# Storing four neighbouring rows of the second-layer weights in a partition, and reading every fourth column of the first layer, in a gated-attention and mixture-of-experts kernel

## The chip, the cores and the metric

One core of a Trainium2 chip. The metric is the device time of one launch in microseconds (us). Versions are compared over executions on the same chip, in alternating rounds.

## The reference

```python
def _attn_ref(q, k, v, f_logit):            # (4, 8, 768, 48) each
    f = 1.0 / (1.0 + np.exp(-f_logit))
    for t in range(S):
        state = f[:, :, t, :, None] * state + np.einsum('bhd,bhe->bhde', k[:, :, t], v[:, :, t])
        y[:, :, t] = np.einsum('bhd,bhde->bhe', q[:, :, t], state)

def _moe_ref(x, domain_probs, w1, w2):      # x (3072, 384), w1 (4, 384, 1024), w2 (4, 1024, 384)
    p = domain_probs / (domain_probs.sum(-1, keepdims=True) + 1e-09)
    for e in range(E):
        h = np.maximum(x @ w1[e], 0.0)
        out += p[:, e:e + 1] * (h @ w2[e])
```

The attention runs in chunks of 128 steps; its output, transposed to `xT`, is the input of the experts. F = 1024 is the hidden width, and any permutation of F is allowed as long as w1's columns and w2's rows agree.

## The kernel before

All weights stay in SBUF as bf16. Row `ko * 128 + ki` of w2 lies in partition `ki`, so one contiguous run is one row: 384 elements, 768 bytes when stored. w1 lies with D in the partitions, and a matmul takes 128 neighbouring columns as stationary operand. The first weights come in pieces: each of the experts 0 and 1 has its w1 in two halves of 512 columns, expert 0 its w2 in two halves too.

```python
    w1_sb = wpool.tile([128, E, KD, F], BF16)
    w2_sb = wpool.tile([128, E, KF, Din], BF16)
    w1_r = moe_w1.rearrange("e (ko ki) f -> e ki ko f", ki=128)
    w2_r = moe_w2.rearrange("e (ko ki) d -> e ki ko d", ki=128)
    # ... cut ...
    def load_w(i, e, which, ks, cols):
        w, r = (w1_sb, w1_r) if which == 1 else (w2_sb, w2_r)
        ins["w", i] = nc.gpsimd.dma_start(out=w[:, e, ks, cols], in_=r[e][:, ks, cols])
    # ... cut ...
    def mm_h(c, e, fc, n0, n1, nf):
        for f in range(nf):
            for kk in range(KD):
                nc.tensor.matmul(out=hp(c, e, fc, n0, n1, nf)[:, f], lhsT=w1_sb[:, e, kk, (fc + f) * 128:(fc + f + 1) * 128],
                                 rhs=tl("xT", c)[:, kk, n0:n1], start=(kk == 0), stop=(kk == KD - 1))
    # ... cut ...
    pieces = [(e, 1, every, slice(i * F // 2, (i + 1) * F // 2)) for e in range(2) for i in range(2)]
    pieces += [(0, 2, slice(i * KF // 2, (i + 1) * KF // 2), every) for i in range(2)]
    pieces += [(e, which, every, every) for e, which in ((2, 1), (1, 2), (3, 1), (2, 2), (3, 2))]
    # ... cut: for every piece i
        op = P.add(f"w {i}", {"DMA": 2.05 if i < 6 else 4.4}, lambda _: None, ..., deps=[iss], lag=1.0)
```

The kernel places its work itself: a plan in Python takes an estimate of each operation's time (the 2.05 and 4.4 us above are such) and fixes the order in which every engine gets its instructions. The waits between engines are set afterwards by the framework, from which tiles and which parts of them each instruction reads and writes.

## Time and profile before

| | before |
|---|---|
| median time | 298.5 us (3 runs), 298.61 us with the runs beside the changed kernel (6) |
| span of the profiled run | 296.6 us |
| TensorE busy | 289.0 us, 97% |
| first w1 matmul, last matmul start | 19.75 us, 292.98 us |
| packets of the queue that loads weights | 11248: 4096 of 768 bytes for w2, 1536 of 1024 and 768 of 2048 bytes for w1 |

In the views, PE is TensorE's matmuls, PEld its weight loads, DVE is VectorE, ACT ScalarE, POOL GpSimd, and q0 the queue that loads the weights. L374 is line 374 of the kernel's file.

TensorE sets the end, so the way to read this profile is by the starts of its matmuls: their spacing, and each place where a spacing is longer than its shape needs. One more piece of the timeline of TensorE matters later, the start of the expert work (start, duration, engine, line, tiles, form, count):

```profile
19.11 0.81 PE L644 MATMUL ps_m<-busy 128*128 128x512 bf16 x3
19.75 0.82 PE L374 MATMUL ps_m<-xT,w_sb 128*128 128x256 bf16 x6
20.41 0.33 PE L365 MATMUL ps_t<-ident,yb 128*128 128x128 bf16 x3
```

Six 256-column matmuls on w1 run without a break, right after three filler matmuls, which work on constant data and whose results nobody reads. The first half of w1 of expert 0 had landed at 19.10 us, the second landed at 21.98 us, and at 19.75 us nothing needs it yet.

### The profile page before, as it was taken

How to read it: one execution, taken by the hardware profiler on the slowest of the kernel's cores; microseconds unless marked ns; L12 is line 12 of the kernel's file. 1: busy time of each engine (PE TensorE's matmuls, PEld its weight loads, DVE VectorE, ACT ScalarE, POOL GpSimd, SP SyncE). 2: the span in 40 equal slices, each digit the busy share in tenths (PEclk: the TensorE clock that was granted, in tenths of full speed). 3: DMA queues.
4: the chain of work that ended last, by engine and by line, in shares of the span. 5: the costliest groups of instructions: out<-in, count | busy, mean ns of one | idle time of the engine just before them, and what ended most of it. 6: DMA issues, size and time to landing. Idle time of an engine off the chain costs nothing.

```text
span 296.6 us, 5591 instructions
## 1 busy us (share of the span) xinstructions
PE 289.0 (97%) x2172; PEld 170.0 (57%) x2172; DVE 126.1 (43%) x250; ACT 174.3 (59%) x317; POOL 106.1 (36%) x180
## 2 busy tenths in 40 slices
PE   6899999999999999999999999999999999999995
PEld 2476555567777775555555555555555555555553
DVE  6786012785763673045375235243523222101223
ACT  5656656666684667777477575554475544465440
POOL 5786401138767448144449372243220000000000
PEclk9999999999999999999999999999999999999999
DMA  7999999998979999998979932102432100200002
GB/s 157 200 169 206 207 192 210 189 210 167 201 152 166 191 171 185 209 187 164 198 133 218 179 60 35 27 0 67 122 61 30 27 2 27 80 2 0 0 2 106
DMA packets 136462, 36.43 MB, mean 123 GB/s; under 512 B 126812, under 2 KB 135644, under 8 KB 136436
## 3 DMA queue, kind: packets, MB, share of 16 engines
q1 hardware_dynamic: 125188, 29.35, 52.0%
q0 software_dynamic: 11248, 6.72, 16.4%
q8 instruction: 17, 0.28, 0.4%
q14 instruction: 9, 0.07, 0.1%
HBM read 31.51 MB, written 4.72 MB: 122 GB/s over the span
## 4 chain that ended last, share of the span: by engine, by line
PE 78%; DMA 14%; POOL 3%; SPq 2%; issue 1%; ACT 1%; DVE 0%; POOLq 0%
PE ps_m L389 37%; PE ps_m L374 35%; DMA w_sb<-in_moe_w_dram 10%; DMA k<-in_k_dram 4%; SPq L237 2%; POOL w_sb L246 2%; PE ps_t L325 2%; PE ps_t L340 1%; PE ps_t L336 1%; PE ps_t L273 1%; POOL vb L233 1%; PE ps_t L346 1%; ACT e L293 1%; DVE o L396 0%; ACT xT L226 0%
## 5 line engine op out<-in xcount | busy, mean ns | idle before, releaser
L385 ACT ACTIVATE h<-ps_m 128x512 bf16<-128x512 f32 (+2 forms) x188 | 102.4, 548 | 91.9 <-PE ps_m L374 88.9
L374 PE MATMUL ps_m<-xT,w_sb 128*128 128x512 bf16 (+3 forms) x708 | 152.8, 339 | 0.6 <-ACT xT L226 0.6
L389 PE MATMUL ps_m<-w_sb,h 128*128 128x384 bf16 (+1 forms) x776 | 152.6, 324 | 0.1
L389 PEld LDWEIGHTS <-h 128*128 128x128 bf16 x776 | 75.0, 98 | 59.0 <-DMA w_sb<-in_moe_w_dram 0.3
L396 DVE SCALAR_TENSOR_TENSOR o<-ps_m,pn,o 128x384 f32<-128x384 f32 (+1 forms) x73 | 44.5, 612 | 117.3 <-PE ps_m L389 111.1
L374 PEld LDWEIGHTS <-w_sb 128*128 128x128 bf16 x708 | 65.3, 98 | 43.5 <-issue 0.7
L301 POOL TENSOR_TENSOR qk<-q,e 128x384 bf16<-128x384 f32 x18 | 21.4, 1195 | 36.5 <-ACT e L293 34.3
L360 POOL TENSOR_TENSOR Sf<-Sf,egs 48x192 f32<-48x192 f32 x40 | 20.2, 504 | 36.5 <-DVE Sf L353 34.4
L329 DVE TENSOR_TENSOR AT<-ps_t,mask 128x512 bf16<-128x512 f32 x48 | 30.2, 683 | 5.1 <-PE ps_t L325 5.1
L383 DVE TENSOR_SCALAR h<-ps_m 128x256 bf16<-128x256 f32 (+2 forms) x40 | 19.3, 499 | 26.5 <-PE ps_m L374 13.1
L293 ACT ACTIVATE e<-ps_t 128x384 f32<-128x384 f32 x48 | 26.7, 668 | 5.0 <-PE ps_t L273 3.5
L301 POOL TENSOR_TENSOR qk<-k,e 128x384 bf16<-128x384 f32 x20 | 20.2, 1013 | 8.7 <-ACT e L293 5.5
L353 DVE TENSOR_TENSOR Sf<-Sf,ps_t 48x192 f32<-48x192 f32 x40 | 14.0, 350 | 10.3 <-PE ps_t L346 9.4
L246 POOL DMA_DIRECT2D w_sb<-in_moe_w_dram x11 | 8.8, 807 | 18.5 <-DMA k<-in_k_dram 17.2
L361 POOL CAST sb<-Sf 48x192 bf16<-48x192 f32 x40 | 13.6, 340 | 2.6
L398 ACT ACTIVATE o<-ps_m,pn 128x384 f32<-128x384 f32 x22 | 12.8, 582 | 2.5 <-PE ps_m L389 1.5
L644 PE MATMUL ps_m<-busy 128*128 128x512 bf16 x34 | 10.9, 423 | 1.5 <-DVE busy L144 1.5
L265 ACT ACTIVATE ex<-f 128x768 f32<-128x768 f32 (+1 forms) x14 | 10.4, 746 | 1.8 <-DMA f<-in_f_logit_dram 1.8
L298 POOL DMA_DIRECT2D egs<-e x16 | 9.0, 563 | 6.9 <-ACT e L293 6.9
L340 PE MATMUL ps_t<-vb,AT 128*128 128x48 bf16 x192 | 11.4, 184 | 0.0
L269 ACT ACTIVATE gp<-ex 128x768 bf16<-128x768 f32 (+1 forms) x14 | 10.5, 751 | 0.3
L340 PEld LDWEIGHTS <-AT 128*128 128x128 bf16 x192 | 9.9, 97 | 1.1
(54 smaller groups left out, 120.6 us busy)
## 6 DMA issues: line engine op xcount, KB each, us to landing
out_dram<-o SPq DMA_DIRECT2D x23, 192.0 KB, 2.0
w_sb<-in_moe_w_dram POOLq DMA_DIRECT2D x5, 768.0 KB, 18.0
k<-in_k_dram SPq DMA_DIRECT2D x10, 384.0 KB, 5.6
q<-in_q_dram SPq DMA_DIRECT2D x10, 384.0 KB, 5.5
v<-in_v_dram SPq DMA_DIRECT2D x10, 384.0 KB, 5.7
f<-in_f_logit_dram SPq DMA_DIRECT2D x9, 384.0 KB, 4.6
w_sb<-in_moe_w_dram POOLq DMA_DIRECT2D x6, 384.0 KB, 9.0
f<-in_f_logit_dram SPq DMA_DIRECT2D x6, 192.0 KB, 3.8
```

Of the source, the lines that this page charges most:

```text
L246: ins["w", i] = nc.gpsimd.dma_start(out=w[:, e, ks, cols], in_=r[e][:, ks, cols])
L293: nc.scalar.activation(out=o, in_=i, func=AF.Exp, scale=1.0 if j else -1.0)
L301: engines[eng].tensor_tensor(out=tl("qk", c, b)[:, j, :, 0:D].rearrange("t (i r) d -> t i r d", r=2), in0=tl("qk"[j], c, b // 2)[:, hh(b), ...
L329: nc.vector.tensor_tensor(out=tl("AT", c, b)[:, r].rearrange("s i t -> s (i t)"), in0=tl("A", c, b, r).rearrange("s i t -> s (i t)"), in1= ...
L340: nc.tensor.matmul(out=y[:, h * D:(h + 1) * D], lhsT=AT[:, r, i, :], rhs=vb[:, h, :], start=(c == 0), stop=True, skip_group_check=True)
L353: nc.vector.tensor_tensor(out=Sf[rows, b], in0=Sf[rows, b], in1=KV[rows, :, r, :], op=ALU.add)
L360: nc.gpsimd.tensor_tensor(out=Sf[rows, b], in0=Sf[rows, b], in1=eg, op=ALU.mult)
L374: nc.tensor.matmul(out=hp(c, e, fc, n0, n1, nf)[:, f], lhsT=w1_sb[:, e, kk, (fc + f) * 128:(fc + f + 1) * 128], rhs=tl("xT", c)[:, kk, n0: ...
L383: nc.vector.tensor_relu(out=dst, in_=src)
L385: nc.scalar.activation(out=dst, in_=src, func=AF.Relu)
L389: nc.tensor.matmul(out=tl("op", c, e, nt, part)[:, cols], lhsT=tl("h", c, e, half_of(c, nt * T))[:, fc, nt * T:(nt + 1) * T], rhs=w2_sb[:, ...
L396: nc.vector.scalar_tensor_tensor(out=o, in0=op, scalar=pe, in1=o, op0=ALU.mult, op1=ALU.add)
```

## The change

The intent is larger packets for w2, so that the weights come sooner: partition `ki` holds the rows `s * 512 + ki * 4 + j`, j = 0 to 3, whose four rows are one run of 3072 bytes. For h to come out in the same order, chunk `fc = 4 s + j` of w1 has to be the columns `s * 512 + j`, `+ 4`, `+ 8` and so on. The plan's estimates change with it. (Here and below an edit is shown in part: unchanged lines and some changed ones are left out, and `...` stands for a part of a line.)

```diff
-    w2_r = moe_w2.rearrange("e (ko ki) d -> e ki ko d", ki=128)
+    w2_r = moe_w2.rearrange("e (s ki j) d -> e ki s j d", ki=128, j=KF // 2)
     def load_w(i, e, which, ks, cols):
-        w, r = (w1_sb, w1_r) if which == 1 else (w2_sb, w2_r)
-        ins["w", i] = nc.gpsimd.dma_start(out=w[:, e, ks, cols], in_=r[e][:, ks, cols])
+        dst, src = w1_sb[:, e, ks, cols], w1_r[e][:, ks, cols]
+        if which == 2:
+            dst = w2_sb[:, e].rearrange("ki (s j) d -> ki s (j d)", j=KF // 2)[:, ks]
+            src = w2_r[e].rearrange("ki s j d -> ki s (j d)")[:, ks]
+        ins["w", i] = nc.gpsimd.dma_start(out=dst, in_=src)
+    def f_cols(fc):
+        s, j = divmod(fc, KF // 2)
+        return slice(s * F // 2 + j, (s + 1) * F // 2, KF // 2)
-                nc.tensor.matmul(..., lhsT=w1_sb[:, e, kk, (fc + f) * 128:(fc + f + 1) * 128],
+                nc.tensor.matmul(..., lhsT=w1_sb[:, e, kk, f_cols(fc + f)],
-    pieces += [(0, 2, slice(i * KF // 2, (i + 1) * KF // 2), every) for i in range(2)]
+    pieces += [(0, 2, slice(i, i + 1), every) for i in range(2)]
-        op = P.add(f"w {i}", {"DMA": 2.05 if i < 6 else 4.4}, ...)
+        op = P.add(f"w {i}", {"DMA": (2.1 if i < 6 else 4.3) if which == 1 else 1.7 if i < 6 else 3.5}, ...)
```

More of the change, by code (lines that the diff above doesn't have):

```diff
@@ L373, in mm_h @@
             for kk in range(KD):
-                nc.tensor.matmul(out=hp(c, e, fc, n0, n1, nf)[:, f], lhsT=w1_sb[:, e, kk, (fc + f) * 128:(fc + f + 1) * 128],
+                nc.tensor.matmul(out=hp(c, e, fc, n0, n1, nf)[:, f], lhsT=w1_sb[:, e, kk, f_cols(fc + f)],
                                  rhs=tl("xT", c)[:, kk, n0:n1], start=(kk == 0), stop=(kk == KD - 1))
@@ L443 @@
                     -600 + 3 * i, deps=issued[-1:] + ([ld[1, "k", 0]] if i == w_last else []))
-        op = P.add(f"w {i}", {"DMA": 2.05 if i < 6 else 4.4}, lambda _: None, -400 if i == w_last else -460 + i, deps=[iss], lag=1.0)
+        op = P.add(f"w {i}", {"DMA": (2.1 if i < 6 else 4.3) if which == 1 else 1.7 if i < 6 else 3.5}, lambda _: None, -400 if i == w_last else -460 + i, deps=[iss], lag=1.0)
         issued.append(iss)
```

## The prediction

In the prediction, rival (a) is that strided weight loads are slow enough to hold up the matmuls.

> **What bounds the kernel now.** I read four views, from coarse to fine. The page first: the busy times, and the span in 40 slices.
>
> ```profile
> span 296.6 us, 5591 instructions
> ...
> PE 289.0 (97%) x2172; PEld 170.0 (57%) x2172; DVE 126.1 (43%) x250; ACT 174.3 (59%) x317; POOL 106.1 (36%) x180
> ...
> PE   6899999999999999999999999999999999999995
> ...
> DMA  7999999998979999998979932102432100200002
> ```
>
> TensorE is busy for 97% of the span, and the DMA engines are nearly full for the first 23 slices of 7.4 us. The change touches both: it makes second-layer weight (w2) transfers cheaper and it alters how TensorE reads first-layer weights (w1). So the question is which of the two sets the end. A busy TensorE may be a slow one, so the next view is the timeline of TensorE in the stage where the weights arrive (start, duration, engine, line, tiles, form):
>
> ```profile
> 34.02 0.81 PE L374 MATMUL ps_m<-xT,w_sb 128*128 128x512 bf16 x3
> 34.67 0.81 PE L389 MATMUL ps_m<-w_sb,h 128*128 128x384 bf16 x4
> 35.32 0.81 PE L374 MATMUL ps_m<-xT,w_sb 128*128 128x512 bf16 x3
> 35.97 0.81 PE L389 MATMUL ps_m<-w_sb,h 128*128 128x384 bf16 x4
> ```
>
> Each group starts 0.65 us after the last: three 512-column matmuls (0.65 / 3 = 216 ns each) or four 384-column ones (162 ns each). The starts of single matmuls in the whole trace give the same medians: 216 ns for 512 columns, 162 for 384, 109 for 256, 56 for 128. That is one column per 0.42 ns in every form[...]. From 19.75 us (first w1 matmul) to 293 us TensorE runs at this pace. Adding up those medians over the order gives 269.3 us against 273.2 measured, so 3.9 us is lost in all. About 2.8 us of that lies around the 48-row attention matmuls of line 325, some 0.11 us at each entry and exit, the same in either kernel. The rest is two waits, in the view of waits (who waited for whom: total us, times, longest):
>
> ```profile
> PE ps_m L374 <- ACT xT L226: 0.6, 1, 0.6
> ...
> PEld L389 <- DMA w_sb<-in_moe_w_dram: 0.3, 1, 0.3
> ```
>
> By start times they cost 0.73 us at 66.6 us and 0.33 us at 58.9 us. The second is the only wait of TensorE for a weight transfer. The chain of waits puts 10% of the span on w transfers, but only because it follows a queue of transfers back from that 0.3 us wait; the other 59 us of that chain were filled with matmuls that had to be done anyway.
>
> [...]No strided bf16 load is in the trace before. Two rows bound it (the last numbers are busy us, mean ns):
>
> ```profile
> L374 PEld LDWEIGHTS <-w_sb 128*128 128x128 bf16 x708 | 65.3, 98 | 43.5 <-issue 0.7
> L340 PEld LDWEIGHTS <-AT 128*128 128x128 bf16 x192 | 9.9, 97 | 1.1
> ...
> L256 PEld LDWEIGHTS ps_m<-ident,praw 24*128 24x128 f32 x4 | 0.6, 207 | 0.4 <-issue 0.4
> ```
>
> The 98 ns is mostly latency: line 340's matmuls, 48 columns each with new weights, start 25 ns apart in a run, so a packed load occupies the array's weight path for at most 25 ns. The third row reads every fourth FP32 column, 16 bytes apart[...]; its load-and-matmul pairs start 120 ns apart. A bf16 load 8 bytes apart should lie between 25 and 120 ns. [...]In the trace w1 of expert 2 lands 3.79 us after the transfer before it and w2 of expert 1 3.83 us after that. Each reads 1.57 MB of FP32 (4 x 393,216 bytes), so both run at 410 GB/s of reads,[...] although one writes 2048-byte and the other 768-byte packets. [...]the packet size hardly shows.
>
> **The change, part by part.**
> 1. w2 packets: 4096 of 768 bytes, mean 79.2 ns, become 1024 of 3072. From 79.2 ns at 768 bytes and 172.6 ns at 2048 (w1), a straight line gives some 247 ns at 3072, an estimate. Summed: 4096 x 79.2 / 16 engines = 20.3 us before and 1024 x 247 / 16 = 15.8 us after, so 1.1 us for each expert's w2. By the landing intervals above it is nearer zero, because packets overlap on an engine. I take 0.2 to 0.5 us an expert. None of it is on TensorE's path except the 0.33 us wait for the last w2.
> 2. w1 weight loads: 708, each beside a running matmul. The 456 of 512 columns give them 216 ns, the 12 of 384 columns 163, the 204 of 256 columns 109, the 36 of 128 columns 56. If a strided load takes 50 ns (half rate), nothing shows. At the bound of 120 ns: 204 x 11 ns + 36 x 64 ns = 4.5 us. I choose nothing, most likely.
> 3. Order: the kernel places its work by its own estimates of transfer times, and these change. The comparison of orders shows the same 2172 matmuls, the first 513 TensorE rows alike, and after them w2 matmuls and the attention of chunk 1 moved forward. Rolling the new order forward with the spacings above, from the same 19.75 us: the second half of w2 of expert 0 is first used at 29.48 us (it landed at 29.75 before), w2 of expert 1 at 37.25 (37.37), the first transposes of chunk 1 at 53.1 instead of 57.0 us (k and q landed at 49.8 and 51.2, and two exponentials and a product of 0.86 us must follow). If the transfers gain nothing, the first two cost up to 0.3 us together, since a wait at the first delays the second as well; with 0.3 us of gain they cost nothing. The last w2 is used later than before, at 59.4 or so, and should no longer be waited for.
>
> Sum: 298.5 - 0.33 (last w2) - 0.2 (part of the 0.73 us wait for xT, as chunk 1 starts earlier) + 0.15 (half of the possible new waits) = 298.1 us.
>
> **The rivals.** (a) [...]For it: [...]no row shows a strided bf16 load. Against: [...]even the FP32 row fits under a 256-column matmul almost. It makes 300 to 303 us; only a load above 216 ns, slower than any in the trace, would touch the 512-column matmuls and cost tens of us. (b) The new order trusts transfers that don't come faster, and TensorE waits for weights or for chunk 1. [...]Against: the needs found above are within 0.3 us of the old landings. It makes 298.5 to 300 us. (c) DMA is the true bound and several us are gained. For it: 14% DMA in the chain and a full DMA row until 170 us. Against: 1.07 us of waits is all that TensorE could get back; it can't make less than 297.3 us unless the first 19.75 us shrink, and the order there is the same and the w2 transfers come later.
>
> **Range and chances.** The three runs before span 1.1 us. With -1.1 us as the most that waits can give, and +2 for a mild form of (a) or (b), 296.9 to 300.2 us should hold it 8 times in 10. Faster by over 2% (below 292.5) needs six times the waits there are: 1%. Slower by over 2% (above 304.5) needs a strided load well above 120 ns: 4%. Within 2%: 95%.
>
> **What would show it.** In the profile after: starts of 512-, 256- and 128-column w1 matmuls still 216, 109 and 56 ns apart (if the latter two grow, (a)); the mean of the w1 weight loads near 98 ns, or longer without effect; 1024 packets of 3072 bytes in place of 4096 of 768, with w2 landings within 0.5 us an expert of before; TensorE's waits for w_sb below 0.3 us, busy time 288 to 290 us. Wrong would be: wider matmul spacing, a wait for w_sb or for chunk 1 above 1 us, or a first w1 matmul that starts elsewhere than near 19.75 us.

## The result, and the profile after

The changed kernel is correct and took 300.47 us in the median of 6 runs (300.04 to 302.63), against 298.61 us before (298.22 to 299.31, 6 runs). The ratio is 1.0082, 95% interval 1.0054 to 1.0109. Ratios here and below are made from the runs of the same rounds, so not quite the ratio of the medians. Two of the six runs, 302.16 and 302.63 us, had a granted clock of 0.994; without them the plain means, 300.34 over 298.68 us, give 1.0056. By the 2% measure it is the same, but it is clear of noise, slower, and 0.27 us above the range that was predicted.

The page of the profile after (span; busy us, share of the span and instructions of each engine):

```profile
span 298.8 us, 5588 instructions
...
PE 289.8 (97%) x2172; PEld 179.8 (60%) x2172; DVE 128.2 (43%) x253; ACT 171.9 (58%) x312; POOL 107.1 (36%) x182
...
q0 software_dynamic: 8176, 6.72, 14.7%
```

The span grew by 2.2 us while TensorE's busy time grew by 0.8 us. The packets came out as planned: 1024 of 3072 bytes with a mean of 257 ns in place of 4096 of 768, so 3072 fewer in the queue. The lost time shows in the view of waits of the changed kernel (who waited for whom: total us, times, longest):

```profile
PEld L382 <- DMA w_sb<-in_moe_w_dram: 2.1, 1, 2.1
...
PE ps_m L382 <- DMA w_sb<-in_moe_w_dram: 1.7, 1, 1.7
...
PE ps_m L382 <- DVE h L391: 0.4, 1, 0.4
```

These are two waits that were not there before (the first two lines are the same one, seen by the weight load and by its matmul). One is for a weight transfer, in w1's line, where before there was none at all. The timeline of TensorE of the changed kernel at the start of the expert work shows the place:

```profile
19.51 0.81 PE L652 MATMUL ps_m<-busy 128*128 128x512 bf16 x3
20.15 0.27 PE L382 MATMUL ps_m<-xT,w_sb 128*128 128x256 bf16 x1
22.16 0.74 PE L382 MATMUL ps_m<-xT,w_sb 128*128 128x256 bf16 x5 [1.74 <-DMA w_sb<-in_moe_w_dram]
```

The group of six is torn: one matmul runs, and the second starts 2.01 us later instead of 0.109. (The 1.74 us in brackets count from the modelled end of the matmul before; costs in this text go by the starts.) In this run the first half of w1 of expert 0 landed at 18.71 us and the second half at 22.11 us. The second matmul waits for the second half, though its columns (every fourth of 0 to 511) all lie in the first. The built programs say so too. These are rows of TensorE's instructions, before and after, with their waits for weight transfers (those for other engines are left out); DMASW3 is the first half, DMASW5 the second:

```
before                                        after
299 L374 Ldweights w_sb [waits DMASW3_49]     299 L382 Ldweights w_sb [waits DMASW3_49]
300 L374 Matmult ps_m_405<-xT_335,w_sb        300 L382 Matmult ps_m_405<-xT_335,w_sb
301 L374 Ldweights w_sb                       301 L382 Ldweights w_sb [waits DMASW5_49]
...
369 L374 Ldweights w_sb [waits DMASW5_49]     369 L382 Ldweights w_sb
```

The pattern suggests why. The second half is a write to columns 512 to 1023 of three rows of 1024 (kk = 0, 1, 2), so it spans the places 512 to 3071 of the tile. The strided read of kk = 0 covers 0 to 508, outside that span, and gets no wait; the one of kk = 1 covers 1024 to 1532, inside the span though it shares no element, and gets one. The contiguous read of kk = 1 before got none. That the framework compares spans when one side is strided is an inference from these rows (and from the same wait at the first group of expert 1, row 481); the wait itself is a fact of the program.

The account of the two profiled runs, by the starts of matmuls: the first w1 matmul starts 0.40 us later (it starts anywhere from 19.35 to 20.48 us in the profiles), the torn group costs 1.90 us, a wait near 84 us for a buffer that VectorE empties costs 0.54 us, and the two waits of before are gone, 0.73 and some 0.23 us. That makes +1.88 of +2.17 us. The rest, 0.3 us, is mostly seven single matmuls on w1, the first after work of another kind, that take 27 or 28 ns longer than their median.

The weight loads themselves did get longer (view of groups with shapes kept apart; the two numbers after the bar are busy us and mean ns):

```profile
L382 PEld LDWEIGHTS <-w_sb 128*128 128x128 bf16 x708 | 75.3, 114 | 38.0 <-DMA w_sb<-in_moe_w_dram 2.1 <-issue 0.5
L397 PEld LDWEIGHTS <-h 128*128 128x128 bf16 x776 | 74.8, 98 | 57.0
```

In the records a load at a step of 4 takes 114 ns; before, it was 98 ns for both groups. But the median spacing of the w1 matmuls is what it was: 216, 109 and 56 ns for 512, 256 and 128 columns.

### The profile page after: what moved, and what is told of

It reads as the page before. It is cut to its first block, busy times and chain, and to the rows that moved or that the text cites. A ratio compares the mean times of both kernels' runs of the same rounds, so it can differ in the third digit from the quotient of the medians. Undisturbed runs are those within 1.5% of the kernel's fastest.

```text
span 298.8 us, 5588 instructions
## 1 busy us (share of the span) xinstructions
PE 289.8 (97%) x2172; PEld 179.8 (60%) x2172; DVE 128.2 (43%) x253; ACT 171.9 (58%) x312; POOL 107.1 (36%) x182
## 4 chain that ended last, share of the span: by engine, by line
PE 91%; DMA 4%; SPq 2%; POOL 1%; DVE 1%; issue 0%; DVEq 0%
PE ps_m L397 42%; PE ps_m L382 42%; DMA w_sb<-in_moe_w_dram 2%; SPq L238 2%; PE ps_t L329 2%; PE ps_t L344 1%; DMA k<-in_k_dram 1%; PE ps_t L340 1%; PE ps_t L350 1%; PE ps_t L277 1%; POOL vb L234 1%; PE ps_t L314 0%; POOL w_sb L250 0%; DVE Sf L357 0%; PE ps_t L369 0%
## 5 line engine op out<-in xcount | busy, mean ns | idle before, releaser
L393 ACT ACTIVATE h<-ps_m 128x512 bf16<-128x512 f32 (+2 forms) x185 | 100.9, 547 | 97.6 <-PE ps_m L382 93.7
L382 PE MATMUL ps_m<-xT,w_sb 128*128 128x512 bf16 (+3 forms) x708 | 154.4, 340 | 2.1 <-DMA w_sb<-in_moe_w_dram 1.7
L382 PEld LDWEIGHTS <-w_sb 128*128 128x128 bf16 x708 | 75.3, 114 | 38.0 <-DMA w_sb<-in_moe_w_dram 2.1
L391 DVE TENSOR_SCALAR h<-ps_m 128x256 bf16<-128x256 f32 (+2 forms) x43 | 21.2, 506 | 18.3 <-PE ps_m L382 16.4
L229 POOL CAST vb<-v 128x384 bf16<-128x384 f32 x18 | 9.7, 566 | 17.2 <-DMA v<-in_v_dram 12.8
L250 POOL DMA_DIRECT2D w_sb<-in_moe_w_dram x11 | 7.8, 718 | 15.1 <-DMA k<-in_k_dram 13.1
L652 PE MATMUL ps_m<-busy 128*128 128x512 bf16 x34 | 11.7, 450 | 1.5 <-DVE busy L144 1.5
```

The source lines that it names most:

```text
L391: nc.vector.tensor_relu(out=dst, in_=src)
L393: nc.scalar.activation(out=dst, in_=src, func=AF.Relu)
```

## The experiments

Theory A: the early wait for the second half of w1 costs the time. Theory B: strided weight loads cost TensorE time elsewhere. Theory C: the new order, made from the new estimates, costs it. Every time is a median of 6 runs (5 for the filler one); "before" was run on the same chip each time, 11 runs, medians 298.80, 298.81 and 298.65 us in the three sets (experiments 1 to 4, 5 to 8, 9 to 11). By the 2% measure every kernel below is the same as before; the differences are tenths of a per cent.

**1. Halves in tiles of their own (removes the wait).**

```diff
-    w1_sb = wpool.tile([128, E, KD, F], BF16)
+    for e in range(E):
+        parts = 2 if e < 2 else 1
+        for i in range(parts):
+            w1_t[e, i] = wpool.tile([128, KD, F // parts], BF16, name=f"w1e{e}h{i}")
```

> The changed kernel, with the halves of w1 of experts 0 and 1 in tiles of their own, so that the second weight load needs no longer wait for the second half. Theory A (the cost is the 1.9 us wait for that half): 298.4 us, 298.0 to 299.0, the first two w1 matmuls 109 ns apart. Theory B (strided weight loads cost TensorE time elsewhere): stays at 300 us or more. Theory C (the new order costs it): stays near 300 us as well.

Measured: correct, 299.34 us, ratio 1.0018 (0.9998 to 1.0039). The group of six runs unbroken (its first two matmuls start 134 ns apart) and 1.1 us of the 1.9 came back, less than the 298.0 to 299.0 us that I expected. The timeline of TensorE of this run says what took the rest:

```profile
28.69 1.46 PE L408 MATMUL ps_m<-w_sb,h 128*128 128x384 bf16 x8
30.55 0.81 PE L408 MATMUL ps_m<-w_sb,h 128*128 128x384 bf16 x4 [0.40 <-DMA w_sb<-in_moe_w_dram]
```

The gap is 0.56 us longer than a matmul: the wait for the second half of w2 of expert 0, which landed at 30.51 us. In the changed kernel that wait is absent, because the torn group had already delayed everything by 1.9 us; taking one wait away uncovers the next. The wait near 84 us is also still here (0.53 us).

**2. The early wait alone, in the kernel before.**

```diff
+                if (c, e, fc + f, n0, kk) == (0, 0, 0, 0, 1):
+                    after(m, ins["w", 1])
```

> The kernel before, with one edit: the second matmul of the first w1 group also waits for the second half of w1 of expert 0. No stride, old packets, old order. Theory A: about 2 us slower than before, 300.2 us (299.8 to 300.9), less up to 0.3 us of the later wait for the last w2, which the delay absorbs. Theories B and C: 298.6 us, as before.

Measured: correct, 300.38 us, ratio 1.0063 (1.0027 to 1.0099). With the layout, packets and order of before (in the built program the wait moves from row 369 to row 301, and no other row of TensorE differs in its waits), this one wait costs 1.58 us by the medians, where the whole change cost 1.86. Its timeline of TensorE is torn in the same way:

```profile
20.48 0.27 PE L374 MATMUL ps_m<-xT,w_sb 128*128 128x256 bf16 x1
22.40 0.72 PE L374 MATMUL ps_m<-xT,w_sb 128*128 128x256 bf16 x5 [1.64 <-DMA w_sb<-in_moe_w_dram]
```

**3. Split tiles, with the order of before.** As 1, with the old estimates (2.05 and 4.4 us). TensorE's order and waits are then row for row those of before; left are stride and packets.

> As the split-tile kernel, but with the transfer estimates of before, so TensorE's order and its waits are row for row those of before; left are the stride and the 3072-byte packets. Theory A: 298.4 us, within 0.5 us of before. Theory B: 300 us or more. Theory C: 298.4 us, while the split-tile kernel is near 300.

Measured: correct, 298.23 us, ratio 0.998 (0.9965 to 0.9996). So without the wait and with the old order the change is a small gain. Against experiment 1, which differs in the order alone, this is 1.1 us less: neither the wait at 30 us nor the one at 84 us is in this trace.

**4. Packets and new order, contiguous columns (wrong result).**

```diff
-lhsT=w1_sb[:, e, kk, f_cols(fc + f)]
+lhsT=w1_sb[:, e, kk, (fc + f) * 128:(fc + f + 1) * 128]
```

> The changed kernel with contiguous w1 columns again (result wrong on purpose): 3072-byte packets and the new order, without stride and without the wait for the second half. Theory A: 298.4 us, as the split-tile kernel. Theory B: 298.4 us, and clearly below the split-tile kernel. Theory C: near 300.5 us.

Measured: 298.15 us, ratio 0.9979 (0.996 to 0.9998). Its wait for the second half of w2 is 0.14 us against 0.56 in experiment 1: w2's second half landed at 30.00 instead of 30.51 us, and by this much such a landing varies between runs. The order's cost therefore varies with it, and C alone doesn't explain the loss. But it is also 1.2 us faster than experiment 1, which has the same order, and that is what theory B had asked for. From the first w1 matmul to the last matmul the two profiles differ by 0.90 us: 0.42 is this wait, 0.23 are two matmuls near 75 us that are not late in the changed kernel with the same stride, and 0.24 at most is left for the stride. The other 0.3 us of the medians is not explained.

**5. Packets alone, in the order of before (wrong result).** As 4, with the old estimates.

> 3072-byte w2 packets alone: contiguous w1 columns (result wrong on purpose), the order and the waits of before. Theory (packets are worth a few tenths of a us, the stride nothing): 298.2 us, ratio to before 0.998, with the wait of 0.3 us for the last w2 gone and w2 landing 0.1 to 0.2 us sooner each. Rival (the gain of the split-tile kernel in the old order came from somewhere else): 298.8 us.

Measured: 298.20 us, ratio 0.9979 (0.9956 to 1.0002). w2 of expert 1 lands 3.74 us after the transfer before it, 3.83 before; the wait for the last w2 is gone from the trace.

**6. The stride alone (wrong result).** Split tiles and strided columns, w2 stored as before, old estimates.

> The stride alone, in split tiles: w2 packets, order and waits of before (result wrong on purpose). Theory (the stride is free at 56 ns spacing and above): as before, 298.8 us, ratio within 0.2% of 1, load rows near 113 ns and spacings 216, 109 and 56 ns. Rival (the stride costs a little that the other runs hid): 0.3% or more slower.

Measured: 298.66 us, ratio 0.9993 (0.9973 to 1.0013). In the order of before the stride costs nothing that timed runs can show, though from the first w1 matmul to the last matmul its profile is 0.5 us longer than that of before (273.75 against 273.23 us), as experiment 3's is 0.4 us longer than 5's. B is out as the cause.

**7. A step of 8 for two experts.**

```diff
-        return w1_t[e, 0][:, kk, f_cols(fc)]
+        return w1_t[e, 0][:, kk, fc:F:KF]          # experts 2 and 3
+            if e >= 2:
+                dst = w2_sb[:, e].rearrange("ki f d -> ki (f d)")
+                src = moe_w2[e].rearrange("(ki f) d -> ki (f d)", f=KF)
```

> As the split-tile kernel in the old order, but experts 2 and 3 keep eight neighbouring F rows in a partition (6144-byte packets) and their w1 columns are read with a step of 8, one bf16 per 16 bytes. Theory (a load has up to 109 ns beside a 256-column matmul): loads of these experts longer than 113 ns in the records, spacing of 256-column matmuls still 109 ns, time as the step-4 kernel, 298.2 us. Rival[...]: 96 of the 256-column matmuls grow by 20 ns or more, 2 us or more slower.

Measured: correct, 299.53 us, ratio 1.0019 (0.9998 to 1.004), some 0.4% worse by ratio than the step of 4 in experiment 3 (another set; the packets of two experts differ too). The view of groups shows step 8 and step 4 side by side:

```profile
L396 PEld LDWEIGHTS <-w1e3h 128*128 128x128 bf16 x168 | 22.7, 145 | 6.6
L396 PEld LDWEIGHTS <-w1e2h 128*128 128x128 bf16 x168 | 21.9, 146 | 6.3
L396 PEld LDWEIGHTS <-w1e0h 128*128 128x128 bf16 x204 | 20.6, 114 | 10.7 <-DMA w1e0h<-in_moe_w_dram 1.1 <-issue 0.9
```

98, 114 and 145 ns for steps 1, 4 and 8. Median spacings stay at 109 and 216 ns, but single matmuls, the first after another kind of work or after a wait, grow by up to 62 ns (216 to 278). Against experiment 3, matmul by matmul, they add up to 0.7 us. So the time was not that of the step of 4, as I had expected, and the loss of 2 us or more that the rival asked for did not come either.

**8. An order between the two.** As 1, with w2 at 1.95 and 3.9 us and w1 at 2.05 and 4.2 us.

> The split-tile kernel with transfer estimates between the two (w2 1.95 and 3.9, w1 2.05 and 4.2 us): the second half of w2 of expert 0 is then first used where it was before, w2 of expert 1 in between. Theory (the new order costs 0.5 us by asking for that half 0.65 us earlier and 0.5 us in a wait near 83 us): the first of these waits is gone, 298.0 to 298.6 us. Rival (order makes no difference, the runs of the split-tile kernel were merely slow): 298.8 to 299.4 us.

Measured: correct, 297.55 us, ratio 0.9963 (0.9938 to 0.9989), faster than both kernels. Its timeline of TensorE asks for the second half of w2 of expert 0 three matmuls later than experiment 1, and nothing waits:

```profile
28.10 1.46 PE L408 MATMUL ps_m<-w_sb,h 128*128 128x384 bf16 x8
29.40 0.81 PE L393 MATMUL ps_m<-xT,w1e1h 128*128 128x512 bf16 x3
30.05 1.46 PE L408 MATMUL ps_m<-w_sb,h 128*128 128x384 bf16 x8
```

**9. The changed kernel again.** 3 of the 12 runs of the changed kernel and of experiment 2 had a granted clock of 0.993 or 0.994 and took 302.2 to 303.4 us.

> The changed kernel unedited, beside the next two on one chip. Theory (the early wait for the second w1 half also lets the granted clock drop in some runs: 3 of the 12 runs of the two kernels with that wait had 0.993 or 0.994 and were 2 to 3 us longer, none of the 64 runs without it): median 300.4 us, one or two of six runs near 302.5 at a clock of 0.994. Rival (the low clocks were chance or belong to a chip): all six at 0.998 or more.

Measured: 300.55 us, ratio 1.0067 (1.0035 to 1.01); one of six runs at 0.994, 303.27 us. But one run of the kernel before in this set had 0.994 as well, at 299.69 us. All told, 4 of 18 runs with the early wait had the low clock, and of the others one of the kernel before, of 33 whose clock is on record, and none of the 48 of experiments 1, 3 to 8 and 11. That points to a link between the wait and the low clock and does not show one.

**10. Fillers in the wait.** The changed kernel with eight matmuls on constant data between the first and the second w1 matmul, to see whether low clocks still come when TensorE works through the wait.

```diff
+                for _ in range(8 if (c, e, fc + f, n0, kk) == (0, 0, 0, 0, 1) else 0):
+                    nc.tensor.matmul(out=spare, lhsT=busy[:, 0:128], rhs=busy, start=True, stop=True)
```

> The changed kernel with eight 512-column filler matmuls (8 x 216 ns = 1.7 us) put between the first and the second w1 matmul, so that TensorE works while it waits. Theory[...]: the same median, 300.4 us, all runs at 0.998 or more. Rival: low clocks in some runs all the same. Six runs can't settle this alone.

Measured: correct, 302.99 us (301.75 to 303.28, 5 runs), ratio 1.0125, all clocks at 0.999 or more. The median missed my expectation by 2.6 us. In its profiled run the second half of w1 landed at 22.89 us, against 22.11 in the changed kernel, and a matmul near 116 us waited 1.2 us for a late gate input. By the starts these two make 0.54 and 1.39 of the 2.3 us by which this profile is longer than that of the changed kernel from the first w1 matmul to the last matmul; why all five runs are slow is not settled. It says nothing firm on the clock either.

**11. Experiment 8 again.**

> The split-tile kernel in the order between the two, once more, on another chip or at another time: 297.6 us again (297.2 to 298.1), ratio to before 0.996 with an interval below 1, no clock below 0.998. Rival (its first result was luck of the transfers): 298.2 to 298.8 us.

Measured: correct, 298.24 us, ratio 0.9977 (0.9953 to 1.0). In its profiled run the first half of w2 of expert 0 landed at 29.62 us, 2 us later than in experiment 8, and TensorE lost 0.90 us to it:

```profile
29.67 1.48 PE L408 MATMUL ps_m<-w_sb,h 128*128 128x384 bf16 x8 [0.74 <-DMA w_sb<-in_moe_w_dram]
```

The gain is there in both, but it is 0.2 to 0.4%, in the second the interval reaches 1, and it rests on landings that vary by as much.

## Why the prediction was wrong

**The step that failed** is part 3, "Order": "The comparison of orders shows the same 2172 matmuls, the first 513 TensorE rows alike". Alike they are in kind and sequence, but not in their waits: row 301 waits for the second half of w1. I then rolled "the new order forward with the spacings above, from the same 19.75 us", and named the needs of the weights by what each matmul reads, not by what the built program makes it wait for. So the sum has no term for this wait, which measured 1.90 us in the changed kernel and 1.6 us of median time alone (300.38 against 298.80 in experiment 2). The view that shows it was to be had: the same comparison, with waits. One of the prediction's own signs of being wrong, "a wait for w_sb or for chunk 1 above 1 us", came true.

**Part 1, packets**: right in kind. I took 0.2 to 0.5 us an expert; the landing interval of w2 of expert 1 fell from 3.83 to 3.67 us (3.74 in experiments 3 and 5), so 0.1 to 0.2, or 2 to 4%. The estimate of 247 ns a packet measured 257. The wait for the last w2 went, as said, worth some 0.2 us and not 0.33: a step out of line 325, which it follows, costs 0.12 us without any wait (and 22 such steps in and out make 2.4 us, not 2.8). Packets do overlap on an engine: in the kernel before, their time was 1.16 times that of the 16 engines in the interval that ends with the landing of w1 of expert 2, and 1.28 times in the next, which ends with w2 of expert 1. The weights arrive in SBUF as bf16, and all transfers of these two intervals moved 205 and 209 GB/s by the trace; no run here shows a limit for that, or for the 410 GB/s of reads. That the packet size hardly shows rests on the landings alone.

**Part 2, strided loads**: right. That the stride would cost nothing was an estimate: the trace before has no strided bf16 load, the bounds of 25 and 120 ns come from two other kinds of load, and the 50 ns of half rate were assumed. The three medians hold, and the load's record grew by 16 ns. What a load occupies is not recorded; that a median spacing of 56 ns holds says only that a step of 4 needs no more than that. (The 25 ns of line 340 are the smallest spacing there; most are 28 or 29.) The profiles show a cost of 0.3 to 0.5 us where I wrote nothing, too little for the timed runs.

**Part 3's other terms**: the wait for `xT` near 66.6 us went fully in the changed kernel (0.73 us; I had taken 0.2). The new order did create waits, as rival (b) put it. The one for the second half of w2, which I placed at 29.48 us and below 0.3 us, measured 0.14 and 0.56 us once the torn group no longer hid it. The one near 84 us, for a buffer emptied by VectorE, 0.53 us, I had not named: I had rolled weights and inputs forward but not the buffers.

**The chances**: within 2% was right. The range failed at its upper end: it had room for a mild form of one rival (2 us above the middle) and the result lay 2.4 us above it. Its lower end was loose too: 298.5 less all 1.07 us of waits is 297.4, not 297.3, and 296.9 takes the waits off a middle from which half of them had gone already.

## What to carry to other kernels

Compare the waits that a change gives each instruction, not only the instructions and their order: a strided view of a tile can bring a wait for a transfer into another part of it (1.90 us here). Where pieces of a tile arrive at different times, give each piece a tile of its own (1.1 of the 1.9 us came back in experiment 1). And when an order is planned from estimates, look at the margin of the tightest need: the order that asked for one half of w2 0.65 us later than experiment 1, and that had no wait near 84 us, was 0.4 to 0.55% faster than it by ratio (experiments 11 and 8), while the larger packets alone gave 0.2%. How much of this is that one use is not shown, and the order of before, in experiment 3, did as well as experiment 11.
